# A fused attention and feed-forward kernel: the odd token tiles of two groups paired, the down weights loaded later, gate sums moved, last stores reordered

## The chip, the cores and the metric

The kernel runs on one core of a Trainium2 chip. The time is device microseconds (us) of one execution. TensorE (PE) multiplies, VectorE (DVE) and ScalarE (ACT) read its results out of PSUM and do elementwise work, GpSimd (POOL) and SyncE (SP) mostly issue DMAs.

## The reference

Eight batches of sigmoid attention feed one gated feed-forward block over all 3584 tokens (8 batches of 448).

```
q, k, v: (8, 12, 448, 64)
scores = q @ k.T / sqrt(64) - log(448)
attn   = sigmoid(scores)
x      = (attn @ v), heads side by side: (3584, 768)
gate   = max(x @ w_gate, 0)        # w_gate: (768, 1536)
val    = x @ w_val                 # w_val:  (768, 1536)
out    = (gate * val) @ w_out      # w_out:  (1536, 768)
```

## The kernel before

**Tiles.** All matmul operands are fp16, sums are fp32 in PSUM. A batch's attention is cut into 21 units: three groups of four heads times seven chunks of 64 keys. A unit (`qk_unit`) is eight matmuls of 64x64 weights (L232) into two PSUM banks and two sigmoids on ACT (L187). After a group's seven units `pv` (28 matmuls, L250) makes two blocks of x transposed, which DVE scales into `xT` (L184). The feed-forward block has two halves: `h = relu(gate) * val` with d_ff on the partitions (tile `hT`, 12 blocks of 128 rows by 896 tokens of two batches, which are called a group), and the "down" product of `hT` with `w_out` (tile `wo`).

**Block products.** Groups 1 to 3 get their gate and val products by a scheme of seven products in place of eight (`gv_pair`, L385): the two batches of a group and the two weight matrices are the blocks. The sums of weights that this needs are `gate_sums` (wg minus wv, written over wv), those per pair of d_ff tiles are `unit_sums`, those of the two batches `batch_sums`. The down product uses the same scheme for a pair of 128-token tiles (`down_pair`, L385): `weight_sums` makes T1 to T4 out of quarters of `wo`, `token_sums` makes S1, S2, S4 and one sum in place out of `hT` (four DVE instructions, L409 and L376). A pair is seven products of six matmuls 128x384. They run in a fixed order on three PSUM banks u, y12 and y11; the first product's bank u is copied out by `first_copy` before the third product adds to it:

```python
product(b, A11, B11)
first_copy(y1[:, lo], b)
beside()
product(c, S1, T1)
...
product(b, S2, T2, False)
```

A group of 896 tokens has seven token tiles, so each group has three pairs and a seventh tile that stands alone: `down` computes it with plain matmuls, 12 of 128x512 and 12 of 128x256 (L346). Batches 0 and 1 (group 0) get gate and val by plain matmuls (`gv`, L309).

**The order of the work.** It is written out by hand. For each batch b the loop over m takes three to five units, then either some `gv` of the queue (`mix`, `hooks`) or, where `mix` is 0, one item of `work` (`next_work`): a `gv_pair` ("w"), a `down_pair` ("y") or a lone tile ("t"). Closures in `jobs` run beside an item. They issue the DVE copies into `rel` with the DMA transposes of the next batch's keys and queries (`dma_transposes`, L215 and L219, issued on SP), the loads of the next batch (POOL), and sums. `prepare` issues the DVE sums of the next item ahead of it. After the last batch the remaining work runs alone. The items of group g are pushed by `push_group` when batch 2g+1 is done: six "w" (groups 1 to 3), the lone tile, the pairs 0, 1, 2; in group 0 pair 0 comes ahead of the lone tile.

**Buffers.** Eight PSUM banks go round in the list `free`; `later` puts an item's banks at the end in the order in which they come free. A matmul into a bank waits for the engine that read it last. `hT` has one buffer, `rel` two, the summed tokens two, the output rows `ysb` four. DVE, ACT, POOL and SP each work through their instructions in order.

**Loads.** POOL issues the loads in the order of the program. `hold(b, g)` is a tiny POOL copy that reads the result of a DMA transpose, so that what POOL issues after it starts after that transpose. At the end of batch 1 `late_loads` issues `hold(2, 1)`, the v of batch 2 and `load_o`, the two loads of `wo` (1536 and 768 KB). The k, q and v of batch 3 follow. `weight_sums` runs in batch 2 at m = 4 and 5, and the pair (0, 0) at the end of batch 2.

Of the kernel before, what the change touches and what calls it, by code (L numbers as in the profile page):

```python
# [17 lines left out]
def kernel(  # L18
# [16 lines left out]
    P = 128  # L35
# [227 lines left out]
    class FirstSlot:  # L263
# [6 lines left out]
        def unit(self, u):  # L270
            qn = self.qn
            cs = range(2 * u, min(2 * u + 2, NCH))
            ps = pairp.tile([P, 2, 512], FP32, tag="pair", name="qk_ps")
            for j, c in enumerate(cs):
                qk(
                    qkT_tiles[(0, self.g)], c, self.c0, self.c1,
                    lambda hh: ps[:, hh, j * qn : (j + 1) * qn],
                )
            i = (self.number * 4 + u) % 12
            PT = early.tile([P, 2, 512], FP16, tag=f"PT{i}", name="PT")  # L280
            n = qn * len(cs)
            sigmoid(PT[:, :, 0:n], ps[:, :, 0:n])
            for j in range(len(cs)):
                self.pieces.append(PT[:, :, j * qn : (j + 1) * qn])

# [16 lines left out]


    def gv(b, q0, qn, f, act_relu):
        ps = []
# [17 lines left out]
        g = b // 2  # L323
        if g not in hT_tiles:
            hT_tiles[g] = hTp.tile([P, NFC, 2 * S], FP16, tag="hT", name="hT")
        o = (b % 2) * S + q0
        nc.vector.tensor_tensor(  # L327
            out=hT_tiles[g][:, f, o : o + qn],
            in0=gate_sb[:, 0:qn],
            in1=ps[1][:, 0:qn],  # L330
            op=AOP.mult,
        )

# [6 lines left out]

    def down(g, t):
        ysb = ysbp.tile([P, DM], FP32, tag="ysb", name="ysb")
        for nm, m0, m1 in (("ya", 0, 512), ("yb", 512, DM)):
            ps = bank(nm)
            for f in range(NFC):
                nc.tensor.matmul(  # L346
                    ps[:, 0 : m1 - m0],
                    hT_tiles[g][:, f, t * P : (t + 1) * P],
                    wo[:, f, m0:m1],
                    start=(f == 0),  # L350
                    stop=(f == NFC - 1),
                )
            nc.vector.tensor_scalar(
                out=ysb[:, m0:m1], in0=ps[:, 0 : m1 - m0], scalar1=OUT_SCALE, scalar2=None, op0=AOP.mult
            )
        store(g, t, ysb, 0, DM, (nc.sync, nc.sync))


# [5 lines left out]
    HF, HM, HD = NFC // 2, DM // 2, NDC // 2  # L364
    late = {}
    sums = {}

    def open_late():
        first_sbuf.close()
        pool = ctx.enter_context(tc.tile_pool(name="late", bufs=1))  # L370
        late["T"] = pool.tile([P, 4, HF, HM], FP16, tag="T", name="T")
        late["X"] = pool.tile([P, 3, HD, S], FP16, tag="X", name="X")
        late["sums"] = ctx.enter_context(tc.tile_pool(name="sums", bufs=2))
# [19 lines left out]


    def weight_sums(i):
        T = [late["T"][:, j] for j in range(4)]
        B11, B21 = wo[:, 0:HF, 0:HM], wo[:, HF:NFC, 0:HM]
        B12, B22 = wo[:, 0:HF, HM:DM], wo[:, HF:NFC, HM:DM]
        sub(T[i], *((B12, B11), (B22, T[0]), (B22, B12), (B21, T[1]))[i])

    def token_blocks(g, p):
        h = hT_tiles[g]
        t1, t2 = (slice(t * P, (t + 1) * P) for t in (2 * p, 2 * p + 1))
        return h[:, 0:HF, t1], h[:, HF:NFC, t1], h[:, 0:HF, t2], h[:, HF:NFC, t2]

# [17 lines left out]
    def down_pair(g, p, beside, then, last, first_copy):  # L423
        A11, A12, S3, A22 = token_blocks(g, p)
        S1, S2, S4 = sums.pop(("y", g, p))
        T1, T2, T3, T4 = (late["T"][:, i] for i in range(4))
        B11, B21, B22 = wo[:, 0:HF, 0:HM], wo[:, HF:NFC, 0:HM], wo[:, HF:NFC, HM:DM]
        y1, y2 = (ysbp.tile([P, DM], FP32, tag="ysb", name="ysb") for _ in range(2))
# [21 lines left out]
        product(b, S3, T3, False)  # L450
        plus(y2[:, hi], b)
        product(c, S4, B22, False)
        plus(y1[:, hi], c)
        if last:
            store(g, 2 * p, y1, 0, DM, (nc.sync, nc.scalar))
        else:
            store(g, 2 * p, y1, 0, DM, (nc.sync, nc.sync))
        then()
        product(b, A22, T4, False)
        scaled_act(y2[:, lo], b)  # L460
        if last:
            store(g, 2 * p + 1, y2, HM, DM, (nc.sync, nc.sync))
            store(g, 2 * p + 1, y2, 0, HM, (nc.sync, nc.scalar))
        else:
            store(g, 2 * p + 1, y2, 0, DM, (nc.sync, nc.sync))

# [30 lines left out]

    def gv_pair(g, f, beside, first_copy):
        x1, x2 = xT_tiles[2 * g], xT_tiles[2 * g + 1]
# [4 lines left out]
        gs = [[gsbp.tile([P, S], FP32, tag="gsb", name="gsb") for _ in range(3)] for _ in range(2)]  # L504
        if g not in hT_tiles:
            hT_tiles[g] = hTp.tile([P, NFC, 2 * S], FP16, tag="hT", name="hT")
        h = hT_tiles[g]
        sets = []
# [22 lines left out]

        def gated(u, o, gate_sb, val):
            nc.vector.scalar_tensor_tensor(
                out=h[:, f + u, o : o + S], in0=gate_sb, scalar=0.0, in1=val, op0=AOP.max, op1=AOP.mult
            )

        product(b, 0, B11)
# [12 lines left out]
        product(b, 2, T4, False)  # L550
        for u in range(2):
            gated(u, 0, gs[u][0][:], b[u][:, 0:S])
        for u in range(2):
            gated(u, S, gs[u][1][:], gs[u][2][:])

# [88 lines left out]
    def late_loads():  # L644
        dma_transposes(2, 1)
        hold(2, 1)
        load_v(2)
        load_o()

# [3 lines left out]
    def push_group(g):  # L653
        tail = [("t", g, 6)] + [("y", g, p) for p in range(3)]
        if g == 0:
            tail.insert(0, tail.pop(1))
        work.extend([("w", g, f) for f in range(0, NFC, 2) if g > 0] + tail)

# [8 lines left out]
    def next_work(jobs=(), alone=False):  # L667
        kind, g, i = work.popleft()

        def beside():  # L670
            for job in jobs:
                job()

        if kind == "y":
            down_pair(g, i, beside, prepare, not work, scaled_act if alone else scaled)
        elif kind == "w":
            gv_pair(g, i, lambda: (prepare(), beside()), nc.scalar.copy if alone else nc.vector.tensor_copy)
        else:
            beside()
            prepare()  # L680
            down(g, i)

    ffn_mix(1, [(1, lambda: both(1, 0))])
    for b in range(1, B):
# [16 lines left out]
        elif b == 2:  # L701
            mix = (2, 2, 1, 1, 1, 2)
            hooks = {
                2: [(0, prepare)],
                4: [(1, lambda: weight_sums(0)), (0, lambda: weight_sums(1))],
                5: [(1, lambda: weight_sums(2)), (0, lambda: weight_sums(3))],
            }
            open_late()
        elif b == 3:
            mix = (1, 1, 1, 0, 0)  # L710
        else:
            mix = (0,) * count
        for m in range(count):
            jobs = []
            for i, (g, c) in enumerate(order[cuts[m] : cuts[m + 1]]):
# [9 lines left out]
                qk_unit(b, g, c)  # L725
            if m == 0 and b > 1:
                jobs.append(lambda: dma_transposes(b, 2))
            if b == 2 and m == count - 1:
                jobs.append(lambda: (dma_transposes(3, 0), dma_transposes(3, 1)))
            elif b == 3 and m == count - 1:  # L730
                jobs.append(lambda: (dma_transposes(4, 0), dma_transposes(4, 1)))
            elif 0 <= m - count + 2 and 3 < b < B - 1:
                jobs.append(lambda: dma_transposes(b + 1, m - count + 2))
            if b == 1:
                if m == 0:
                    load(2, 0, 1, "kq")
                    load(2, 1, 2, "kq")
                    load(2, 2, 3, "kq")
            elif m == 0 and b + 1 < B:
                if b == 3:  # L740
                    jobs.append(lambda: hold(3, 2))
                jobs.append(lambda: (load(b + 1, 0, 3, "kq"), load_v(b + 1)))
            if b % 2 and b > 2:
                if m == count - 1:
                    jobs.append(lambda: (batch_sums_t1(b // 2), batch_sums(b // 2, (0, 1))))
            elif b > 3 and m == 0:
                jobs.append(lambda: batch_sums(b // 2 - 1, (1, HD)))
            if b == 2 and m == count - 1:
                ffn_mix(mix[m], hooks[m])
                next_work(jobs)  # L750
            elif mix[m]:
                for job in jobs:
                    job()
                ffn_mix(mix[m], hooks.get(m, ()))
            else:
                next_work(jobs)
            if b == 3 and m == 3:
                for f in range(0, NFC, 2):
                    gate_sums(f, f + 2)
    pv_finish(B - 1)  # L760
    push_group(B // 2 - 1)
    next_work([lambda: batch_sums(B // 2 - 1, (1, HD))])
    while work:
# [31 lines left out]
```

## Time and profile before

| what | value |
|---|---|
| time, median of 3 runs | 401.66 us (400.9 to 402.0) |
| the profiled execution | 400.93 us, span of its trace 399.2 us |
| PE busy | 388.9 us, 97% |
| DVE busy | 279.9 us, 70% |
| ACT busy | 223.0 us, 56% |
| POOL busy | 49.4 us, 12% |
| granted TensorE clock | 0.999 |
| DMA written by queue | loads 23.33 MB, transposes and stores 19.24 MB |

The span is from the first to the last instruction in the trace of one execution; the time of a run is a little longer. A busy engine in this table is one with an instruction in it: matmuls are pipelined, so PE's share says little on its own, and the places where PE waits have to be looked up in its timeline. In the timeline, a row is a run of like instructions with start, length and, in brackets, the idle time ahead of it with the instruction that ended it.

### The profile page before, as it was taken

To read this page: it belongs to the slowest core of one execution; us is meant where nothing else is said; L and a number is where in the kernel's file an instruction comes from. 1 tells how busy PE (TensorE), PEld (TensorE's weight loads), DVE (VectorE), ACT (ScalarE), POOL (GpSimd) and SP (SyncE) were. 2 spreads that over 40 slices of the span, in tenths; PEclk is the share of its full clock that TensorE was granted. 3 is DMA by queue.
4 is the path that set the end of the run, shared out by engine and by line. 5 is a ranking of instruction groups with operands and counts; after the bars stand their busy time and mean duration, and the time that the engine had idled before them with its cause. 6 is when DMAs were issued, how large, how long until landed. Compare 5 with 4: busy or idle time off the path is not lost.

```text
span 399.2 us, 8737 instructions
## 1 busy us (share of the span) xinstructions
PE 388.9 (97%) x3488; PEld 217.9 (55%) x3488; DVE 279.9 (70%) x539; ACT 223.0 (56%) x475; POOL 49.4 (12%) x73
## 2 busy tenths in 40 slices
PE   8999999999998999999999999999999999999994
PEld 3678786545455554554555555455455555555562
DVE  2454344367358889999758889999766779887661
ACT  5946778783885565655665455565566234533131
POOL 8643301600030300003000300000000000000000
PEclk9999999999999999999999999999999999999999
DMA  9999994999897894224945695223012320000144
GB/s 149 199 199 204 205 141 94 177 203 187 178 161 152 165 204 76 46 48 51 178 85 133 130 218 89 48 24 61 12 40 80 80 79 2 0 2 0 39 115 124
DMA packets 68793, 43.69 MB, mean 109 GB/s; under 512 B 35856, under 2 KB 65296, under 8 KB 68752
## 3 DMA queue, kind: packets, MB, share of 16 engines
q0 software_dynamic: 30736, 23.33, 39.1%
q1 hardware_dynamic: 37584, 19.24, 23.0%
q8 instruction: 27, 0.44, 0.5%
q10 hardware_dynamic: 432, 0.56, 0.4%
q14 instruction: 14, 0.11, 0.1%
HBM read 47.19 MB, written 11.01 MB: 146 GB/s over the span
## 4 chain that ended last, share of the span: by engine, by line
PE 73%; DMA 14%; issue 6%; POOL 3%; DVE 2%; ACT 1%; ACTq 0%; POOLq 0%; DVEq 0%
PE u L385 32%; PE g L385 15%; PE y L385 9%; DMA v<-in_v_dram 6%; PE qk_ps L232 5%; PE pv_ps L250 5%; DMA wo<-in_moe_w_out_dram 4%; DMA k<-in_k_dram 4%; PE ya L346 3%; PE v_ps L309 1%; PE yb L346 1%; PE g_ps L309 1%; POOL q L110 1%; POOL k L110 1%; DVE wv L376 1%
## 5 line engine op out<-in xcount | busy, mean ns | idle before, releaser
L187 ACT ACTIVATE PT<-qk_ps 128x448 f16<-128x448 f32 (+3 forms) x318 | 150.6, 594 | 71.2 <-PE qk_ps L232 71.1
L385 PEld LDWEIGHTS <-S 128*128 128x128 f16 x540 | 52.8, 98 | 44.4 <-issue 0.8
L528 DVE TENSOR_TENSOR gsb<-g,gsb 128x448 f32<-128x448 f32 x72 | 43.0, 625 | 14.5 <-PE g L385 13.8
L232 PE MATMUL qk_ps<-qkT 64*64 64x448 f16 (+2 forms) x756 | 50.0, 336 | 0.9 <-DVE qkT L206 0.5
L421 ACT ACTIVATE ysb<-u 128x384 f32<-128x384 f32 x27 | 13.4, 498 | 56.3 <-PE u L385 56.3
L327 DVE TENSOR_TENSOR hT<-gate_sb,v_ps 128x256 f16<-128x256 f32 (+2 forms) x36 | 16.2, 465 | 33.5 <-ACT gate_sb L318 22.4
L385 PEld LDWEIGHTS <-hT 128*128 128x128 f16 x288 | 27.7, 98 | 21.0 <-issue 3.2
L524 ACT COPY gsb<-u 128x448 f32<-128x448 f32 x48 | 25.8, 566 | 23.9 <-PE u L385 22.9
L250 PE MATMUL pv_ps<-PT,v 64*64 64x448 f16 (+2 forms) x756 | 37.4, 329 | 0.4 <-issue 0.4
L184 DVE TENSOR_SCALAR xT<-pv_ps 128x448 f16<-128x448 f32 (+2 forms) x53 | 27.9, 567 | 13.4 <-PE pv_ps L250 12.1
L232 PEld LDWEIGHTS <-qkT 64*64 64x64 f16 x756 | 20.3, 105 | 24.9 <-issue 16.3
L309 PE MATMUL v_ps<-xT,wv 128*128 128x256 f16 (+2 forms) x216 | 33.3, 291 | 0.4 <-DVE hT L327 0.2
L309 PE MATMUL g_ps<-xT,wg 128*128 128x256 f16 (+2 forms) x216 | 33.5, 292 | 0.1
L385 PEld LDWEIGHTS <-wv 128*128 128x128 f16 x216 | 21.1, 98 | 19.8
L385 PEld LDWEIGHTS <-wg 128*128 128x128 f16 x216 | 20.3, 98 | 20.6 <-issue 3.0
L250 PEld LDWEIGHTS <-v 64*64 64x64 f16 x756 | 21.8, 107 | 11.8 <-issue 1.4
L385 PE MATMUL u<-T,hT 128*128 128x384 f16 x144 | 27.3, 326 | 0.0
L437 DVE SCALAR_TENSOR_TENSOR ysb<-y,ysb 128x384 f32<-128x384 f32 x24 | 13.4, 557 | 18.8 <-PE y L385 11.3
L110 POOL DMA_DIRECT2D k<-in_k_dram x14 | 10.9, 779 | 112.3 <-DVE rel L215 105.8
L309 PEld LDWEIGHTS <-wg 128*128 128x128 f16 x216 | 18.5, 98 | 11.5 <-issue 5.0
L309 PEld LDWEIGHTS <-wv 128*128 128x128 f16 x216 | 20.1, 98 | 8.2 <-DMA wv<-in_moe_w_val_dram 0.5
L385 PE MATMUL u<-xT,wg 128*128 128x448 f16 x108 | 23.5, 353 | 0.1
(67 smaller groups left out, 531.3 us busy)
## 6 DMA issues: line engine op xcount, KB each, us to landing
out_dram<-ysb SPq DMA_DIRECT2D x53, 192.0 KB, 2.9
k<-in_k_dram POOLq DMA_DIRECT2D x5, 672.0 KB, 11.8
q<-in_q_dram POOLq DMA_DIRECT2D x5, 672.0 KB, 14.9
v<-in_v_dram POOLq DMA_DIRECT2D x8, 336.0 KB, 15.6
v<-in_v_dram POOLq DMA_DIRECT2D x16, 168.0 KB, 15.3
k<-in_k_dram POOLq DMA_DIRECT2D x8, 224.0 KB, 10.4
wo<-in_moe_w_out_dram POOLq DMA_DIRECT2D x1, 1536.0 KB, 13.2
q<-in_q_dram POOLq DMA_DIRECT2D x6, 224.0 KB, 11.3
```

The costliest lines, as they stand in the source:

```text
L110: nc.gpsimd.dma_start(t16[:, xs, cs], rows_of(src, b)[:, xs, cs])
L184: nc.vector.tensor_scalar(out=xT, in0=src, scalar1=XSCALE, scalar2=None, op0=AOP.mult)
L187: nc.scalar.activation(PT_ap, ps_ap, AF.Sigmoid, bias=sig_bias, scale=qk_scale)
L232: nc.tensor.matmul(out_of(hh)[o : o + 64, :], qkT[rows, c, cols], qkT[rows, NCH + c0 : NCH + c1, cols], start=True, stop=True, tile_positi ...
L250: nc.tensor.matmul(ps[hh][64 * r : 64 * r + 64, 0:qn], v16[rows, 2 * g + hh, c * D : (c + 1) * D], pieces[c][rows, hh, :], start=(c == 0), ...
L309: nc.tensor.matmul(ps[-1][:, 0:qn], wt[:, dc, f * P : (f + 1) * P], xT_tiles[b][:, dc, q0 : q0 + qn], start=(dc == 0), stop=(dc == NDC - 1),)
L327: nc.vector.tensor_tensor(out=hT_tiles[g][:, f, o : o + qn], in0=gate_sb[:, 0:qn], in1=ps[1][:, 0:qn], op=AOP.mult,)
L346: nc.tensor.matmul(ps[:, 0 : m1 - m0], hT_tiles[g][:, f, t * P : (t + 1) * P], wo[:, f, m0:m1], start=(f == 0), stop=(f == NFC - 1),)
L385: nc.tensor.matmul(ps[:, 0:n], A[:, k_, :], W[:, k_, :], start=(first and k_ == 0), stop=(k_ == kn - 1), skip_group_check=True,)
L421: nc.scalar.activation(o, ps[:, 0:HM], AF.Copy, scale=OUT_SCALE)
L524: by(gs[u][i][:], ps[u][:, 0:S])
L528: nc.vector.tensor_tensor(out=gs[u][i][:], in0=ps[u][:, 0:S], in1=gs[u][i][:], op=AOP.add)
```

## The change

1. **Pairing.** The seventh token tiles (tile 6) of groups 0 and 1, and of groups 2 and 3, form a pair of the block scheme. For an even group, the part of h that belongs to tile 6 (tokens 768 to 895) is written into a tile `aside` in place of `hT`. One gating instruction of DVE becomes two there (320 and 128 columns). `down` is gone. Group 0 and 2 have the pairs 0, 1, 2; groups 1 and 3 the pairs 3, 0, 1, 2, where pair 3 is the new one.
2. **End of a group's gates.** In the last `gv_pair` of a group the sums of the next pair are issued between the two halves of the gating: after the even batch's half in groups 0 and 2, after the odd batch's half in groups 1 and 3.
3. **Weight sums.** T3 is written over its quarter of `wo`, so T has three blocks. T1 and T2 are summed at the end of m = 2 in batch 3, T3 and T4 beside the pair (0, 0), which now runs at m = 3 of batch 3.
4. **Down weights.** `load_o` moves from the end of batch 1 to m = 4 of batch 2, behind k, q, v of batch 3 and a `hold(3, 1)`. The transposes of batch 3 move ahead into m = 4 and 5 of batch 2, and `hold(3, 2)` ahead of batch 4's loads is dropped.
5. **Gate sums.** They ran in a row at m = 3 of batch 3. Now four pieces of six run at the end of batch 2 and of m = 0 in batch 3, the last two beside an item at m = 0 of batch 4.
6. **Last stores.** In the last pair the right half of y2 is stored before y1.
7. Pool sizes: the sigmoid tiles of the first slots get buffers of their own or share those of the later units.

```diff
+    ASIDE = 6 * P
+    def gated(g, f, o, n, gate_sb, val, relu=AOP.max):
...
+        cut = max(o, min(end, ASIDE)) if g % 2 == 0 else end
+        for a, z, dst in ((o, cut, hT_tiles[g]), (cut, end, late.get("aside"))):
+            if a < z:
...
-    def down(g, t):
...
-        sub(T[i], *((B12, B11), (B22, T[0]), (B22, B12), (B21, T[1]))[i])
+        T1, T2, T4 = (late["T"][:, j] for j in range(3))
+        sub(*((T1, B12, B11), (T2, B22, T1), (B12, B22, B12), (T4, B21, T2))[i])
...
+        if p == 3:
+            return late["aside"][:, 0:HF], late["aside"][:, HF:NFC], h[:, 0:HF, t1], h[:, HF:NFC, t1]
...
         plus(y2[:, hi], b)
+        if last:
+            store(*to2, y2, HM, DM, (nc.sync, nc.sync))
         product(c, S4, B22, False)
         plus(y1[:, hi], c)
...
+        even_first = final is None or final[1] % 2 == 0
+        for even in (even_first, not even_first):
+            for u in range(2):
+                if even:
+                    gated(g, f + u, 0, S, gs[u][0], b[u])
+                else:
+                    gated(g, f + u, S, S, gs[u][1], gs[u][2])
+            if final and even is even_first:
+                final[0]()
...
         dma_transposes(2, 1)
         hold(2, 1)
         load_v(2)
-        load_o()
...
-        tail = [("t", g, 6)] + [("y", g, p) for p in range(3)]
-        if g == 0:
-            tail.insert(0, tail.pop(1))
-        work.extend([("w", g, f) for f in range(0, NFC, 2) if g > 0] + tail)
+        work.extend([("w", g, f) for f in range(0, NFC, 2) if g > 0])
+        work.extend([("y", g, p) for p in ((3, 0, 1, 2) if g % 2 else (0, 1, 2))])
...
-                4: [(1, lambda: weight_sums(0)), (0, lambda: weight_sums(1))],
-                5: [(1, lambda: weight_sums(2)), (0, lambda: weight_sums(3))],
+                5: [(0, lambda: (gate_sums(0, 2), gate_sums(2, 4)))],
...
+            hooks = {
+                0: [(0, lambda: (gate_sums(4, 6), gate_sums(6, 8)))],
+                2: [(0, lambda: (weight_sums(0), weight_sums(1)))],
+            }
...
+            if b == 2 and m == 4:
                 jobs.append(lambda: (dma_transposes(3, 0), dma_transposes(3, 1)))
+                jobs.append(lambda: (hold(3, 1), load_o()))
+            elif b == 2 and m == 5:
+                jobs.append(lambda: dma_transposes(3, 2))
...
+            elif b == 3 and m == 3:
+                jobs.append(lambda: (weight_sums(2), weight_sums(3)))
+            elif b == 4 and m == 0:
+                jobs.append(lambda: (gate_sums(8, 10), gate_sums(10, 12)))
...
-                if b == 3:
-                    jobs.append(lambda: hold(3, 2))
...
-            if b == 3 and m == 3:
-                for f in range(0, NFC, 2):
-                    gate_sums(f, f + 2)
     pv_finish(B - 1)
-    push_group(B // 2 - 1)
-    next_work([lambda: batch_sums(B // 2 - 1, (1, HD))])
+    batch_sums(B // 2 - 1, (1, HD))
     while work:
         next_work((), True)
```

## The prediction

> **What bounds the kernel now.** I read the page first, then PE's timeline from end to end, then DVE's and POOL's where PE waits or where the change puts something. All durations are of the profiled execution[...]. Changes are summed against the span and added to the median.
>
> ```profile
> PE 388.9 (97%) x3488; PEld 217.9 (55%) x3488; DVE 279.9 (70%) x539; ACT 223.0 (56%) x475; POOL 49.4 (12%) x73
> ```
>
> PE is occupied nearly all the time. Whether it is at its pace shows in the starts of successive rows. At the end of group 1's gates:
>
> ```profile
> 197.86 0.57 PE L232 MATMUL qk_ps<-qkT 64*64 64x448 f16 x8
> 198.26 1.49 PE L250 MATMUL pv_ps<-PT,v 64*64 64x448 f16 x28
> 199.59 0.55 PE L232 MATMUL qk_ps<-qkT 64*64 64x448 f16 x8
> 200.07 2.76 PE L346 MATMUL ya<-wo,hT 128*128 128x512 f16 x12
> 202.67 1.47 PE L346 MATMUL yb<-wo,hT 128*128 128x256 f16 x12
> 204.07 0.96 PE L232 MATMUL qk_ps<-qkT 64*64 64x448 f16 x16
> ```
>
> Twelve 128x512 take 2.60 us from start to start, 216.7 ns each. A product of a pair (six 128x384) takes 0.975 us, a pair 6.83. So PE sets the end almost everywhere. The exceptions lie in batches 2 and 3:
>
> ```profile
> 90.08 1.30 PE L309 MATMUL v_ps<-xT,wv 128*128 128x448 f16 x6 [0.20 <-DVE hT L327]
> ...
> 96.17 1.14 PE L385 MATMUL u<-T,S 128*128 128x384 f16 x6 [0.57 <-DVE ysb L416]
> ...
> 123.14 1.14 PE L385 MATMUL u<-wo,hT 128*128 128x384 f16 x6 [1.16 <-DVE xT L184]
> ```
>
> By start-to-start these stops cost more than the brackets say: 0.36, 0.73 and 1.22 us, 2.3 in all. Behind the first two stand the sums of `wo` on DVE, which waited for its load; behind the third the six gate sums (2.9 us on DVE at 119.66):
>
> ```profile
> 68.31 0.17 POOL L638 COPY gate<-qkT 1x2 f16<-1x2 f16 x1 [19.42 <-DMA qkT<-rel]
> 70.90 2.08 POOL L164 DMA_DIRECT2D wo<-in_moe_w_out_dram  x2
> ...
> 88.14 1.36 DVE L376 TENSOR_TENSOR T<-wo 128x2304 f16<-128x2304 f16 x1 [1.75 <-DMA wo<-in_moe_w_out_dram]
> ```
>
> And DVE at the end of group 1's gates, where the change turns the order round:
>
> ```profile
> 196.34 1.19 DVE L528 TENSOR_TENSOR gsb<-g,gsb 128x448 f32<-128x448 f32 x2
> 197.44 1.14 DVE L533 SCALAR_TENSOR_TENSOR hT<-gsb,u 128x448 f16<-128x448 f32 x2
> 198.51 1.15 DVE L533 SCALAR_TENSOR_TENSOR hT<-gsb 128x448 f16<-128x448 f32 x2
> 199.79 1.16 DVE L184 TENSOR_SCALAR xT<-pv_ps 128x448 f16<-128x448 f32 x2
> 200.87 0.55 DVE L409 TENSOR_TENSOR S<-hT 128x768 f16<-128x768 f16 x1
> ...
> 202.51 0.55 DVE L376 TENSOR_TENSOR hT<-hT 128x768 f16<-128x768 f16 x1
> 202.98 0.68 DVE L353 TENSOR_SCALAR ysb<-ya 128x512 f32<-128x512 f32 x1
> ```
>
> The reader is to see that DVE runs without a gap, that two gatings take 1.07 us and the four token sums 2.11 (200.87 to 202.98), and that only the first gating row reads the PSUM bank u.
>
> [...] the trace has 216.7 and 162.5, so a column costs the same in either scheme. [...] DVE stood at 88.14 for `wo` with a gating ready behind it, and PE stopped at 90.08 for that gating. [...] Here the first packet comes 1.6 to 1.9 us after the issue starts (109.50 to 111.09, 68.79 to 70.68), and the T sum starts 1.3 us after the last packet of `wo` (86.84 to 88.14).
>
> **The change, step by step.**
>
> *Pairing.* Four lone tiles at 3.90 us (2.60 + 1.30) go, two pairs at 6.83 come: -15.6 + 13.66 = **-1.95 us**, all on PE.
>
> *wo and batch 2/3.* The three stops of before go: **-2.3**. Pair (0, 0) moves behind batch 3's m = 2, so PE reaches m = 0 of batch 3 at 93.2 in place of 101.13, and the pair, where the lone tile now starts at 115.21, at 107.2. When is `wo` there? DVE reads xT until 86.3, then makes the four copies (0.30 each). SP issues transpose (3, 0) at 87.1 and (3, 1) 1.7 later (as at 96.78 and 98.47 now), 88.8. One transpose moves 2.3 us of packets and starts 1.2 after its issue (104.88, 106.07 to 108.38), so the second ends at 92.9 and is seen at 93.3. The hold and its hand-over take 0.54 (108.96 to 109.50): `wo` is issued at 93.9, packets from 95.7, 11.7 us of them (75.2 to 86.8 in the trace of before), the sum at 108.7. That is 1.5 us after PE has reached the pair. T1 takes 1.28 (88.14 to 89.42), so the second product starts at 110.0 in place of 108.2 (1.8 lost). T2 and then the copy of bank u stand ahead of the third: 111.8 in place of 111.0 (0.8). T3 and T4 (2.6) end at 114.3, before the fifth and seventh product need them. Sum **+2.6**. If `wo` came in time, T1, T2 and the copy alone would cost 1.0; each us later adds one. Bounds +1.0 and +4.5 (3 us late). Queued behind the hold on POOL are batch 4's loads, needed only from 120 on. The copies of (3, 2) find both `rel` taken and hold DVE until (3, 0) lands at about 91; behind them stand two gatings and two gate sums, and the first gating ends near 92.3, while PE comes back to its bank at 93.6: 0.
>
> *Gate sums.* Four pieces of 0.48 fall where DVE has gaps of 1 to 3 us (after 95 and 98): 0. The last two stand in batch 4, m = 0, ahead of the reading of y11 and u (136.38 to 137.9 now), and the seventh product at 138.12 waits for u: **+0.3**, between 0 and 0.5.
>
> *End of group 1.* The odd gatings run at 197.44 to 198.51, the sums to 200.62, the even ones, which free the two u banks, to 201.69. By the order of `free`, the third of the four units behind `gv_pair` takes these banks, and the order of the changed program has it wait for the even gating; PE is there at 199.59. It goes on at 201.8: **+2.2**. Everything of PE stands behind it. Bounds 1.5 (if the sums go faster) and 2.4.
>
> *End of group 2.* The even gatings end at 290.15 as now. Then come the sums (2.11), four odd pieces in place of two (1.20; 320 and 128 columns scaled from 448 at 0.535, with 0.07 fixed), xT (1.08) and the pair's copy of u (0.47): done at 295.0. The pair starts at 291.71 as the lone tile did, and its third product is due at 293.66: **+1.4**, bounds 0.9 and 1.7. Now the lone tile has no such copy.
>
> *End of group 3.* There are no units between. Odd gatings 368.98 to 370.04, S1 0.58 later; the second product is due at 370.28: **+0.45**, bounds 0.2 and 0.7.
>
> *Stores.* Now the last of SP's six half stores is issued at 395.72, since two of y2's right half stand at 394.07 and 394.71. Moved ahead (their data is there at 392.55), the last is issued with ACT's at 394.68: **-0.95**, bounds -0.5 and -1.1.
>
> *At nothing:* the split gatings of group 0 (+0.07 each beside DVE's gaps), tile `aside` as weights, T3 in place (same size), buffers of the sigmoid tiles (PE's and ACT's rows show no wait for one). The last batch's sums now stand behind pv without a pair beside them: T2 is ready about 1.9 us after pv's end, and the third product of the pair, whose first two take 2.27, comes later.
>
> Sum: -1.95 - 2.3 + 2.6 + 0.3 + 2.2 + 1.4 + 0.45 - 0.95 = **+1.75 us**, so 403.4.
>
> **Rivals.**
> Faster: *the two waits at the group ends are hidden*, because another bank than u is taken or the copy runs before the sums. For it: PE had no stop at these ends before, although DVE ran without a gap. Against it: the order of the changed program names just these waits. The point that decides is whether the even gating is over when PE reaches the third unit at 199.59. Without 2.2, 1.4 and 0.45 the sum is -2.3: 399.4.
> No change: *`wo` arrives in time* (its transfer is alone in the queues, the transposes land early), which takes 1.6 off: +0.15, 401.8. The point is a T1 start before 107.
> Slower still: *`wo` comes late by three more us*[...]: 406. Against it: batch 3's loads end at 84.5 by the sizes.
> *The pairs save nothing*: excluded, since the changed program has 42 matmuls of 384 columns per pair.
>
> **How the numbers follow.** A difference under about 0.3% (1.2 us) is what a measurement of this kernel can't tell from none. My forecast has 0.6 (slower by over 0.3% in 0.5 of it, within in 0.1), its bounds make 401.7 to 405.2. Arrival in time has 0.17, the hidden waits 0.15, late `wo` 0.08. Range 400.6 to 405.3: it takes in the second and all but the far ends of the others. Faster 0.15, same 0.27, slower 0.58.
>
> **What would show it.** Right: rows of the third unit after the gates of group 1 waiting some 2.2 us for DVE hT, a 1.4 us wait of PE for DVE ysb in the first pair of group 2, T1 released by the `wo` DMA near 108.7 with PE waiting behind it, and a last store issue 1 us after the last product, not 2. Wrong: PE going through both ends as it does now, or T1 starting right behind the last gating of batch 1.

## The result, and the profile after

| | before | after |
|---|---|---|
| time, median | 401.4 us (400.9 to 402.0, 4 runs) | 407.67 us (406.47 to 408.57, 4 runs) |
| ratio, 95% interval | | 1.0154 (1.0117 to 1.0190) |
| span of the profiled execution | 399.2 us | 406.3 us |

The change makes the kernel 1.5% slower. I had forecast the direction, but +1.75 us where +6.3 came in the median and +7.1 in the profiled spans, outside my range. All runs below are given as ratios to the kernel before, measured on the same chip as the run; differences between two runs are differences of these ratios.

The page after, busy times and the row of granted TensorE clock in 40 slices:

```profile
PE 390.1 (96%) x3476; PEld 217.4 (53%) x3476; DVE 285.0 (70%) x570; ACT 226.5 (56%) x482; POOL 49.5 (12%) x73
...
PEclk9999999999989999999999999999999999999999
```

PE has 12 matmuls fewer and yet 1.2 us more of busy time, and one slice has a lower clock. PE's timeline, at pair (0, 0), at the end of batch 3, and at the ends of groups 1, 2 and 3:

```profile
107.81 1.15 PE L384 MATMUL u<-wo,hT 128*128 128x384 f16 x6
112.12 1.73 PE L384 MATMUL y<-T,S 128*128 128x384 f16 x6 [3.16 <-DVE T L375]
113.98 2.08 PE L384 MATMUL u<-T,S 128*128 128x384 f16 x6
...
119.90 0.57 PE L232 MATMUL qk_ps<-qkT 64*64 64x448 f16 x8
...
131.03 0.57 PE L232 MATMUL qk_ps<-qkT 64*64 64x448 f16 x8 [1.17 <-DMA qkT<-rel]
...
202.53 0.34 PE L232 MATMUL qk_ps<-qkT 64*64 64x448 f16 x1 [1.67 <-DVE hT L319]
203.06 0.57 PE L232 MATMUL qk_ps<-qkT 64*64 64x448 f16 x7 [0.18 <-DVE hT L319]
...
301.69 1.14 PE L384 MATMUL u<-T,S 128*128 128x384 f16 x6 [1.43 <-DVE ysb L418]
...
374.89 1.15 PE L384 MATMUL y<-T,S 128*128 128x384 f16 x6 [0.34 <-DVE S L411]
```

The second product waits 3.16 us for T1. Then the starts lie 1.86 and 1.87 us apart in place of 0.975: the trace's record of the granted clock has 0.5 for 3.4 us from here. From 107.81 to 119.90 the pair takes 12.09 us where a pair without waits takes 6.92 to the first matmul of the unit behind it (6.83 to another pair): 5.2 us too many. The wait at 131.03 I did not foresee. By start-to-start the stops at the group ends cost 2.4, 1.6 and 0.5 us, and none was there before. What the second product waited for, on POOL and DVE:

```profile
93.75 0.17 POOL L636 COPY gate<-qkT 1x2 f16<-1x2 f16 x1 [18.74 <-DMA qkT<-rel]
94.21 2.07 POOL L164 DMA_DIRECT2D wo<-in_moe_w_out_dram  x2 [0.28 <-issue]
...
110.70 1.36 DVE L375 TENSOR_TENSOR T<-wo 128x2304 f16<-128x2304 f16 x1 [3.26 <-DMA wo<-in_moe_w_out_dram]
```

The issue came 0.3 us after the time where I put it (93.9), the sum 2.0 us after (108.7). And DVE at the end of group 1, where the gating that frees the bank `u` now stands behind the four token sums:

```profile
198.55 1.15 DVE L319 SCALAR_TENSOR_TENSOR hT<-gsb 128x448 f16<-128x448 f32 x2
199.73 0.56 DVE L411 TENSOR_TENSOR S<-hT 128x768 f16<-128x768 f16 x1
...
201.39 0.55 DVE L375 TENSOR_TENSOR hT<-aside,hT 128x768 f16<-128x768 f16 x1
201.86 1.14 DVE L319 SCALAR_TENSOR_TENSOR hT<-gsb,u 128x448 f16<-128x448 f32 x2
```

### The profile page after: what moved, and what is told of

Same layout as the page of the kernel before. It is cut to its first block, busy times and chain, and to the rows that moved or that the text cites. A ratio compares the mean times of both kernels' runs of the same rounds, so it can differ in the third digit from the quotient of the medians.

```text
span 406.3 us, 8744 instructions
## 1 busy us (share of the span) xinstructions
PE 390.1 (96%) x3476; PEld 217.4 (53%) x3476; DVE 285.0 (70%) x570; ACT 226.5 (56%) x482; POOL 49.5 (12%) x73
## 4 chain that ended last, share of the span: by engine, by line
PE 82%; DMA 6%; DVE 6%; ACT 3%; issue 1%; POOL 0%; ACTq 0%; DVEq 0%; POOLq 0%
PE u L384 31%; PE g L384 14%; PE y L384 9%; PE qk_ps L232 7%; PE pv_ps L250 6%; PE g_ps L333 6%; PE v_ps L333 5%; DMA wo<-in_moe_w_out_dram 4%; DMA qkT<-rel 3%; ACT PT L187 2%; DVE gsb L526 2%; PE warm_ps L175 1%; DVE hT L319 1%; PE trt L201 1%; DVE T L375 1%
## 5 line engine op out<-in xcount | busy, mean ns | idle before, releaser
L384 PEld LDWEIGHTS <-S 128*128 128x128 f16 x576 | 56.5, 98 | 52.6 <-DVE T L375 3.5
L423 ACT ACTIVATE ysb<-u 128x384 f32<-128x384 f32 x32 | 15.9, 497 | 62.8 <-PE u L384 62.3
L384 PEld LDWEIGHTS <-hT 128*128 128x128 f16 x312 | 30.0, 98 | 22.0 <-issue 3.1
L319 DVE SCALAR_TENSOR_TENSOR hT<-gate_sb,v_ps 128x256 f16<-128x256 f32 (+2 forms) x36 | 14.6, 420 | 33.1 <-ACT gate_sb L342 22.6
L184 DVE TENSOR_SCALAR xT<-pv_ps 128x448 f16<-128x448 f32 (+2 forms) x53 | 27.8, 566 | 13.1 <-PE pv_ps L250 12.2
L440 DVE SCALAR_TENSOR_TENSOR ysb<-y,ysb 128x384 f32<-128x384 f32 x28 | 15.6, 557 | 22.3 <-PE y L384 15.1
L384 PE MATMUL u<-wo,hT 128*128 128x384 f16 x156 | 29.7, 326 | 0.1
## 6 DMA issues: line engine op xcount, KB each, us to landing
v<-in_v_dram POOLq DMA_DIRECT2D x8, 336.0 KB, 15.1
```

The costliest lines, as they stand in the source:

```text
L184: nc.vector.tensor_scalar(out=xT, in0=src, scalar1=XSCALE, scalar2=None, op0=AOP.mult)
L319: nc.vector.scalar_tensor_tensor(out=dst[:, f, a - d : z - d], in0=gate_sb[:, a - o : z - o], scalar=0.0, in1=val[:, a - o : z - o], op0=relu,
L384: nc.tensor.matmul(ps[:, 0:n], A[:, k_, :], W[:, k_, :], start=(first and k_ == 0), stop=(k_ == kn - 1), skip_group_check=True,)
L423: nc.scalar.activation(o, ps[:, 0:HM], AF.Copy, scale=OUT_SCALE)
L440: nc.vector.scalar_tensor_tensor(out=o, in0=ps[:, 0:HM], scalar=OUT_SCALE, in1=o, op0=AOP.mult, op1=AOP.add)
```

## The experiments

Every kernel is the changed kernel with the edit shown. The theory is that two things make the loss: the down weights (`wo`) come late, with a half clock behind the wait, and VectorE's order of work at the group ends. The rivals are named in each expectation.

### fill: work for TensorE during the wait

```diff
         beside()
+        if (g, p) == (0, 0):
+            for _ in range(15):
+                nc.tensor.matmul(a[:, 0:S], wg[:, 0, 0:P], wg[:, 0, 0:S], start=True, stop=True)
         product(c, S1, T1)
```

> Adds 15 matmuls of 128 columns by 448 between the first and the second product of pair (0,0), into the bank that the third product overwrites: TensorE has work while it waits for the sums T1, and the rest is the changed kernel. The fifteen take 2.8 us at 0.19 each, less than the wait of 3.2. Theory A (the clock fell to half because TensorE stood idle for 3.2 us): the second and third products take 0.975 us each, a gain of 1.8 us, near 405.9. Rival B (the clock falls for another reason, the load at that place): the products stay near 1.86 us each and the time near 407.7.

Ratio 1.0139 (1.0119 to 1.0159). The granted clock is 1.00 from 105 to 119 us, and the second and third product take 1.14 us each in place of 1.73 and 2.08: theory A, as with work in place of the idle time the clock did not fall. But the third product now waits 0.72 us for VectorE's copy of u, which had lain hidden in the slow products, so the pair has 4.0 us too many in place of 5.2, and the gain in the median can't be told from nothing.

### reorder: a product without weight sums goes second

```diff
         beside()
+        if (g, p) == (0, 0):
+            product(a, A12, B21)
+            plus(y1[:, lo], a)
         product(c, S1, T1)
...
-        product(a, A12, B21)
-        plus(y1[:, lo], a)
+        if (g, p) != (0, 0):
+            product(a, A12, B21)
+            plus(y1[:, lo], a)
```

> In pair (0,0) alone the product A12 B21, which needs no sum of the weights and only the first of the two weight transfers, is issued second instead of fourth, ahead of S1 T1. Theory A (the loss there is the wait for T1, and the half clock follows from the length of the idle time): one product of 0.975 us fills a third of the wait, which falls from 3.16 to near 2.2 us; if that is short enough, the products behind it take 0.975 us each; the gain is 1.0 us from the wait and 1.8 from the clock, together 2.8, near 404.5. Rival B (2.2 us idle still lowers the clock): a gain of 1.0, near 406.3. Rival C (the first product of B21 waits for its weights too): no gain, 407.3.

Ratio 1.0182 (1.0147 to 1.0217): no gain. PE's timeline:

```profile
111.44 1.14 PE L384 MATMUL y<-T,S 128*128 128x384 f16 x6 [2.15 <-DVE T L375]
113.31 2.08 PE L384 MATMUL u<-T,S 128*128 128x384 f16 x6 [0.72 <-DVE ysb L418]
115.96 2.08 PE L384 MATMUL u<-wo,hT 128*128 128x384 f16 x6 [0.58 <-ACT ysb L423]
```

The wait for T1 fell to 2.15 us as expected, and the product behind it ran at full pace. Then came waits of 0.72 and 0.58 us, and the granted clock was 0.66 on average from 112.1 to 115.5 and 0.50 from there to 119.0. Rival B is nearest: in this execution the clock fell although no wait in the pair was longer than 2.15 us.

### wo_early: the weights ahead of batch 3's v

```diff
-                jobs.append(lambda: (hold(3, 1), load_o()))
+                pass
...
-                jobs.append(lambda: (load(b + 1, 0, 3, "kq"), load_v(b + 1)))
+                if b == 2:
+                    jobs.append(lambda: (load(3, 0, 3, "kq"), load_o(), load_v(3)))
+                else:
+                    jobs.append(lambda: (load(b + 1, 0, 3, "kq"), load_v(b + 1)))
```

> The down weights are issued in batch 2, m = 0, behind batch 3's k and q and ahead of its v, with no hold by work of the chip; all else as in the changed kernel. Theory A (the late weights cost most of the loss: the wait of 3.2 us ahead of the second product, and the half clock that follows it): the sums T1 start right behind the last gating, near 107 us; pair (0,0) takes about 1.0 us more than a dense pair instead of 5.2; the second and third products take 0.975 us each; the kernel gains about 4.2 us, to near 403.5. If the wait of 1.17 us for the transpose into (4,0) goes too, near 402.3. Rival B (the half clock comes of the block products themselves, not of the wait): the wait goes but the two products stay at 1.86 us, near 405.5. Rival C (v of batch 3 and the transpose (3,0) now come late behind 1.6 MB of weights): a wait of 1 us or more in batch 3's first chunk gives part of it back, 404 to 406.

Ratio 1.0362 (1.0335 to 1.0389), 8 us worse than the changed kernel, far beyond rival C. Pair (0, 0) lost its wait (0.9 us too many), but:

```profile
102.70 0.96 PE L232 MATMUL qk_ps<-qkT 64*64 64x448 f16 x8 [9.67 <-DMA qkT<-rel]
```

The packets of the transposes (3, 0) and (3, 1) now lay among those of `wo` and v and took from 90.67 to 103.67, 13.0 us in place of 4.5. The rows behind the 9.7 us of idle time are slow (the first takes 0.96 us for eight matmuls that take 0.57 elsewhere, the next 3.47 for 28 that take 1.49), and the page's row of the granted clock has 7 tenths in its two slices from 93.2 to 114.0.

### late32: the third transpose behind the weights

```diff
-            if m == 0 and b > 1 and b != 3:
+            if m == 0 and b > 1:
...
-            elif b == 2 and m == 5:
-                jobs.append(lambda: dma_transposes(3, 2))
```

> The transpose (3,2) goes back to batch 3, m = 0, behind the issue of the down weights, as in the kernel before; all else as in the changed kernel. Theory A (the packets of (3,2), 93.65 to 97.04, went ahead of the weights and cost them 1.1 to 1.3 us): the weights' packets start near 95.9 and end near 108; T1 starts 1.2 us earlier, near 109.4, and the wait falls to about 2 us; gain 1.2, or 3.0 with the half clock gone: 404.3 to 406.1. Rival B (the packets of (3,2) now lie among those of the weights and delay them as much): no gain or a loss, 407 to 408.5. The transpose itself is needed only near 120, so no wait for it is expected.

Ratio 1.0237 (1.0207 to 1.0266): rival B, and more. The weights' packets start at 95.72 as expected but end at 112.5. The time from issue to landing of the five transposes in this stretch (minimum, median, maximum):

```profile
DMA to landing us min/median/max: 4.1/4.6/14.9
```

The transpose (3, 2) took 14.9 us where it takes 5.2 in the changed kernel, and I had its due time wrong: it is needed at 106.9, not 120, and PE waited for it:

```profile
112.08 0.96 PE L232 MATMUL qk_ps<-qkT 64*64 64x448 f16 x8 [5.21 <-DMA qkT<-rel]
```

From 95 to 113 us the queue of the transposes moved 1824 packets and 0.46 MB, almost all of them this transpose's, and the load queue 3263 packets and 2.50 MB. Why the transpose took so much longer beside the loads was not shown.

### rel3: the three transposes issued together

```diff
-        rel = relp.tile([P, TW, P], FP16, tag="rel", name="rel")
+        if (b, g) == (3, 2):
+            rel = late["T"][:, 2].rearrange("p x y -> p (x y)")[:, 0 : TW * P].rearrange(
+                "p (c x) -> p c x", x=P
+            )
+        else:
+            rel = relp.tile([P, TW, P], FP16, tag="rel", name="rel")
...
-                jobs.append(lambda: (dma_transposes(3, 0), dma_transposes(3, 1)))
+                jobs.append(lambda: (dma_transposes(3, 0), dma_transposes(3, 1), dma_transposes(3, 2)))
...
-            elif b == 2 and m == 5:
-                jobs.append(lambda: dma_transposes(3, 2))
```

> All three transposes into batch 3 are issued together in batch 2, m = 4: the third one's source is put into the tile of the weight sums, which is unused until T1 is made, so that VectorE's copies for it need not wait 2.52 us for the buffer of (3,0). The hold and the weights stay behind (3,1). Theory A (the weights come late because (3,2)'s packets go ahead of them, and those come late because of the buffer): (3,2)'s packets end near 95.5 instead of 97.0, the weights' packets end near 107.8, T1 starts near 109.2, 1.5 us earlier than in the changed kernel, the wait falls to 1.7 us, and if that leaves the clock at full speed the gain is 1.5 + 1.8 = 3.3: near 404. Rival B (the clock still falls): a gain of 1.5, near 405.8. Rival C (the weights' packets start no earlier, because their own issue after the hold sets them): 407.

Ratio 1.0180 (1.0165 to 1.0194): no gain, the time of rival C but not its reason. Counted from the issue of (3, 0), the third transpose is issued 1.0 us earlier, but its packets end only 0.5 earlier (7.9 us for all three, one after another) and T1 starts 0.2 earlier. The weights' packets do start 0.9 earlier, but they take 13.6 us in place of 12.5. So the wait for the buffer was not what made T1 late; why these packets take longer stays open.

### wo_in_time: the arrival altered alone

With the source of (3, 2) in T as in the run before:

```diff
                 2: [(0, prepare)],
+                3: [(0, lambda: (dma_transposes(3, 0), dma_transposes(3, 1), hold(3, 1)))],
...
-                jobs.append(lambda: (dma_transposes(3, 0), dma_transposes(3, 1), dma_transposes(3, 2)))
-                jobs.append(lambda: (hold(3, 1), load_o()))
+                jobs.append(lambda: (dma_transposes(3, 2), load_o()))
```

> The changed kernel with one thing altered: the transposes into batch 3 and, behind them, the down weights start earlier (transposes (3,0), (3,1) and the hold at the end of batch 2, m = 3, (3,2) with its source in the unused tile T and the weights at m = 4). The pair, the gatings, the copies and the stores stay as changed. Theory A (my step put at +2.6 is the whole of the error, and its rest with weights in time is 1.0, from T1, T2 and the copy of u ahead of the third product): T1 starts right behind the last gating, near 107.2; the pair takes 1.0 to 1.4 us more than a dense one in place of 5.2, no half clock; gain 3.8 to 4.2, near 403.3, and 402.2 if the wait for the transpose into (4,0), 1.2 us, is gone in it. Rival B (the clock falls, or the wait comes back elsewhere): over 405.

Ratio 1.0068 (1.0043 to 1.0094), 403.81 us: theory A, with a gain of about 3.5 us where it had 3.8 to 4.2. PE in pair (0, 0):

```profile
106.80 1.15 PE L389 MATMUL u<-wo,hT 128*128 128x384 f16 x6
108.05 1.15 PE L389 MATMUL y<-T,S 128*128 128x384 f16 x6
109.91 1.14 PE L389 MATMUL u<-T,S 128*128 128x384 f16 x6 [0.71 <-DVE ysb L423]
```

All three transposes' packets are over at 92.6, the weights' start at 93.4 and T1 at 106.63, 15.1 us after their issue in place of 16.5. The pair has 1.15 us too many, of which my step put 1.0, and in this execution the granted clock is 1.0 on average. The wait for the transpose into (4, 0) is still there, with 0.6 us.

### gates, and both

```diff
-        even_first = final is None or final[1] % 2 == 0
+        even_first = final is None or final[1] != 3
...
-            if final and even is even_first:
+            if final and even is (final[1] == 1) ^ even_first:
                 final[0]()
...
-            down_pair(g, i, beside, prepare, not work, scaled_act if alone else scaled)
+            down_pair(g, i, beside, prepare, not work, scaled_act if alone or (g, i) in ((1, 3), (2, 0)) else scaled)
```

> In the run of work at the end of group 1 both gatings (even and odd rows) go ahead of the token sums on VectorE, and the first copy of u in pairs (1,3) and (2,0) is made by ScalarE instead of VectorE. Theory A (the two stops at the ends of groups 1 and 2 are VectorE's order of work): the stop at the end of group 1 falls from 2.3 to about 0.35 us and that at the end of group 2 from 1.6 to about 0.35, and the kernel gains 2.8 to 3.2 us, near 404.7. Rival B (the sums are then late for the second product of the pair): the stop moves behind the first product and the gain at group 1 is under 0.5 us; together under 1.8, 406 or more.

Ratio 1.0064 (1.0047 to 1.0081), 3.6 us better than the changed kernel: theory A. PE at the end of group 1 no longer stops:

```profile
200.04 1.49 PE L250 MATMUL pv_ps<-PT,v 64*64 64x448 f16 x28
201.37 0.55 PE L232 MATMUL qk_ps<-qkT 64*64 64x448 f16 x8
201.85 1.15 PE L384 MATMUL u<-wo,aside 128*128 128x384 f16 x6
```

Of both stops about 0.35 us is left, ahead of the third product. So at the end of group 1 the sums were not needed as early as the changed kernel makes them; the gating was. At the end of group 2 the edit leaves the order of the gatings as it is, and the copy by ScalarE alone takes the stop away.

> The early down weights and the new order of the gatings with ScalarE's copies together. Theory A (the two causes are independent and add): 4.2 + 3.0 us less than the changed kernel, near 400.3, or 399.3 if the wait for the transpose into (4,0) goes too: 0.3 to 0.5% faster than the kernel before. Rival (one wait hides in the other, or a new one opens): 402 to 404.

The same edit on top of wo_early: 1.0277 (1.0258 to 1.0296), 3.4 us better than wo_early alone, about as much as on the changed kernel. The gain at the group ends does not depend on the weights; the rest of this run is wo_early's loss, with a wait of 9.0 us for the transpose (3, 0).

### stores_old: the last stores as before

```diff
-        if last:
-            store(*to2, y2, HM, DM, (nc.sync, nc.sync))
         product(c, S4, B22, False)
...
         if last:
+            store(*to2, y2, HM, DM, (nc.sync, nc.sync))
             store(*to2, y2, 0, HM, (nc.sync, nc.scalar))
```

> In the last pair the halves of y2 are stored in the order of the kernel before, both behind its last product, and all else is as in the changed kernel. My prediction put the reordering at 0.95 us of gain, so this should lose 0.95: near 408.2. The rival, from the traces (5.23 us from the last product's start to the end instead of 5.64): it loses 0.4, near 407.7, because the last transfer's landing and not the issue ends the kernel.

Ratio 1.0150 (1.0131 to 1.0170), not to be told from the changed kernel. The trace resolves it: from the last product's last matmul (the expectation calls it the product's start) to the end of the span it is 5.61 us here and 5.64 before, and 5.20 to 5.30 in the other kernels. The reordering is worth 0.4. The last issue does come 1.0 us earlier (1.16 us after that matmul in place of 2.2), but the last packet ends only 0.45 earlier (3.8 in place of 4.24).

### best1, best3, best3e, best4: can it beat the kernel before?

best1 has the edits of gates, reorder and late32:

> Three edits together: the new order of the gatings with ScalarE's copies (3.4 us in its own run), A12 B21 second in pair (0,0), and the transpose (3,2) behind the down weights. Theory A (independent costs that add): 407.3 - 3.4 - 2.8 - 1.2 = 399.9 or a little less, 0.3% faster than the kernel before. Rival (the transpose among the weights' packets takes back what the reordering gives, or the wait for the transpose into (4,0) stays at 1.2 us): 402 to 403.5.

1.0133 (1.0114 to 1.0151): late32's 5.2 us wait is in it, so the sum failed at that term. best3 has gates, reorder and rel3, with ScalarE's copy in pair (0, 0) too:

> The run with the three transposes issued together, and besides it A12 B21 second in pair (0,0), the gatings' new order at the end of group 1, and ScalarE for the first copy of u in pairs (0,0), (1,3) and (2,0). Theory A: 3.4 us from the ends of groups 1 and 2; in pair (0,0) a wait of about 0.7 us for T1 stays and the half clock goes, so that 4 of its 5.2 us are gained: 407.3 - 3.4 - 4.0 = 399.9, 0.3% under the kernel before. Rival (the half clock stays, as with A12 B21 alone): 402.5.

1.0030 (1.0018 to 1.0042), 402.26 us. The wait for T1 was still 2.16 us, since T1 came no sooner after the issue than in rel3, though in the profiled execution the clock stayed at full (1.00 from 105 to 119 us). best3e puts wo_in_time in rel3's place:

> As the run before it, but (3,0), (3,1) and the hold move from batch 2, m = 4, to the end of m = 3, about 1.6 us earlier on VectorE (85.1 instead of 86.76), and (3,2) and the weights follow at m = 4. Theory A: the weights come 1.0 to 1.6 us earlier still, T1 before the second product is due; no wait in pair (0,0): 0.7 to 1.0 us better than the run before it, near 399. Rival B (the transposes now lie among the packets of batch 3's v, which end at 86.6, and take two to three times as long): nothing gained or a loss of 1 us.

0.9964 (0.9954 to 0.9975), 399.45 us: theory A. It beats the kernel before by 0.36%. T1 starts at 107.01 and the pair has 1.1 us too many. best4 is best3e without reorder:

> As the fastest run so far (weights in time, gatings in the new order, ScalarE's copies), but with the products of pair (0,0) in the changed kernel's order again: with T1 there in time, A12 B21 second is not needed, and its 0.58 and 0.19 us of waits for ScalarE's copies should go. Theory: the second product waits some 0.3 us for T1 and the third 0.3 for T2; 0 to 0.3 us better than that run, 399.2 to 399.5. Rival: T1 is later than the second product by 0.8 or more, 400.

0.9960 (0.9947 to 0.9974), the same within the intervals. Its pair has 1.3 us too many, with waits of 0.34 us for T1 and 0.65 for ScalarE's copy; reorder is worth nothing once the weights are there. So the early weights and the two edits at the group ends, with ScalarE's copy in pair (0, 0), are together worth 7.8 us of the changed kernel's time, where wo_in_time and gates alone gave 3.5 and 3.6.

## Why the prediction was wrong

| step | predicted | in the trace after |
|---|---|---|
| pairing | -1.95 | -1.95 (pairs of 6.83 without waits) |
| stops of before gone | -2.3 | gone |
| `wo` late at pair (0, 0) | +2.6 | +5.2 |
| gate sums, batch 4 | +0.3 | +0.1 |
| pair (0, 1), seventh product | not in the sum | +0.25 |
| end of group 1 | +2.2 | +2.4 |
| end of group 2 | +1.4 | +1.6 |
| end of group 3 | +0.45 | +0.5 |
| stores | -0.95 | -0.4 |
| wait for the transpose into (4, 0) | not in the sum | +1.2 |
| start, a wait near 22 us | 0 | +0.5 |

The right column sums to the 7.1 us. The wait near 22 us is not the change's: 0.37 us before and 0.90 after, it lies between 0.37 and 1.25 us in the other kernels, whose start is the same.

**The step that failed** is the late `wo`. Its order of events was right: the hold, the issue, DVE at T1, and PE behind it, and wo_in_time confirms its rest of 1.0. Two sizes were wrong. I let the weights' packets start 1.8 us after their issue and run alone, though I had a third transpose issued just ahead of them: 3.4 us of packets, which the edit itself put there. The weights' packets started 2.8 us after the issue, when those were over, and 1.8 in late32, where the transpose was not there yet. T1 came 16.5 us after the issue, where I had 14.8; with the transposes out of the way it is 15.1. (I also misread the trace before: the last packet of `wo` ends there at 87.77, not at 86.84. From its first packet to T1 it is 13.1 us, near the 13.0 of my sum, so this cost nothing.) And I priced the wait by its length only. The half clock behind it made the next two products 1.8 us longer, a cost that hid the 0.8 I had put there for the copy of u. In four profiled executions with this code of the pair it has 4.4 to 6.0 us too many: two slowed products in three of them, and three, of 1.90 to 1.92 us, in gates, where it is 6.0.

**The wait for the transpose into (4, 0)** has no place in my prediction; of batch 4 I had looked at the loads alone. SP's issue took 2.81 us in place of 1.53 and the packets came in two pieces. It appears in the profiled executions of some of the kernels and not of others, with the issue at 2.6 to 2.8 us where PE waits and 1.5 to 2.3 where it does not. What lengthens that issue stays open.

**Stores:** I took the last issue for the last landing. Here ACT's and SP's last stores are issued at the same moment (402.23 and 402.22) behind y1's, and the later of them lands 3.0 us after its issue, where the last one before took 2.4.

**The group ends** came out within 0.2 us each, and gates undoes those of groups 1 and 2. Of the rivals, hidden waits is refuted by the brackets; the one with `wo` three us later than in my sum was right that it comes later, by 2.0 us in the trace, and its 406 is nearest. My range of 400.6 to 405.3 shut out both of them, at 399.4 and 406, though it was said to leave out only far ends.

## What to carry to other kernels

In this kernel a late buffer cost its wait and, where TensorE had nothing else to do, in several profiles also the clock behind it: 3.16 us of waiting for T1 and then 1.8 us for two slowed products. With the wait filled (fill) or avoided (wo_in_time) the profiles have a clock of 1.00 there; with a wait of 2.15 us (reorder) the clock fell, with one of 2.16 us (best3) it did not. So fill or avoid such a wait, and don't count on shortening it. When a transfer is moved, list what each of the DMA queues has in flight at that time. Here transposes beside bulk loads came late (13.0 us in place of 4.5 for two in wo_early, 14.9 in place of 5.2 to the landing of one in late32), and in late32 so did the load (16.8 us of packets in place of 12.5); the remedy that worked was to let the transposes end first and start everything earlier. Where an engine takes its instructions in the order of the program, as VectorE does in these timelines, put the work that frees a bank ahead of the work that prepares later operands: VectorE's gating at 201.86 stood behind four token sums and TensorE stopped for 1.67 us, and the other order, with ScalarE's copies, was worth 3.6 us in gates.

## What the runs showed of the hardware

**The clock behind a wait.** The profiles show the half clock behind some of TensorE's waits, and full clock behind others of the same length:

| profile, place | waits of TensorE, us | products from start to start, us, or granted clock |
|---|---|---|
| after, pair (0, 0) | 3.16 | 1.86 and 1.87, in place of 0.975 |
| rel3, pair (0, 0) | 2.97 | 1.90 and 1.58 |
| stores_old, pair (0, 0) | 2.93 | 1.89 and 1.37 |
| gates, pair (0, 0) | 2.88 | 1.90, 1.92 and 1.92 |
| reorder, pair (0, 0) | 2.15, 0.72, 0.58 | clock 0.66 from 112.1 to 115.5, 0.50 to 119.0 |
| best3, pair (0, 0) | 2.16, 0.26, 0.58 | clock 1.00 from 105 to 119 |
| fill, pair (0, 0) | 0.72, the wait for T1 filled | clock 1.00 from 105 to 119 |
| late32, end of group 1 | 1.67, 0.18 | clock 0.54 from 206.0 to 209.4 |
| wo_early, end of group 1 | 1.67, 0.19 | clock 0.68 from 209.4 to 212.8, 0.80 to 216.0 |
| after, end of group 1 | 1.67, 0.18 | clock 1.00 from 200 to 210 |

PE's rows at the end of group 1 in late32, where a product takes up to 1.92 us from start to start:

```profile
204.88 0.57 PE L232 MATMUL qk_ps<-qkT 64*64 64x448 f16 x7 [0.18 <-DVE hT L319]
205.38 1.78 PE L384 MATMUL u<-wo,aside 128*128 128x384 f16 x6
206.96 2.13 PE L384 MATMUL y<-T,S 128*128 128x384 f16 x6
```

So in these profiles the length of a wait alone did not decide. What else does was not shown, nor whether the clock makes the spread of the changed kernel's runs (2.1 us, against 1.1 before).
